# Threshold attention and MLP mixer in one kernel: the residual is turned at the third product and moved every iteration, the ring of turned e gets a fifth place, e two tiles, and the half group adds its residual last

## The chip, the cores and the metric

The kernel runs on one core of one Trainium2 chip. Its time is device time in microseconds (us), from the start of the program to its end. The core has five engines that take their instructions from queues of their own, in order, and wait for each other through semaphores: TensorE (PE; PEld is its loading of weights, which overlaps), VectorE (DVE), ScalarE (ACT), GpSimd (POOL) and SyncE (SP, which here only issues transfers). ACT issues transfers too. An instruction that waits holds back all that stand behind it in its queue.

## What is computed

Eight batches, eight heads, 576 tokens, head size 64. Attention keeps only the scores that lie within tau of the row's maximum; its output goes into a mixer: a product over tokens with a residual, then a product over channels with a residual.

```python
scores = scale * np.matmul(q, k.transpose(0, 1, 3, 2))
thresh = np.max(scores, axis=-1, keepdims=True) - tau
scores = np.where(scores >= thresh, scores, -1000000000.0)
scores = scores - np.max(scores, axis=-1, keepdims=True)
attn = np.exp(scores)
attn = attn / (np.sum(attn, axis=-1, keepdims=True) + 1e-09)
attn_out = np.matmul(attn, v)
x = attn_out.transpose(0, 2, 1, 3).reshape(B, S, H * D)
u = x + (np.maximum(x.transpose(0, 2, 1) @ w_tok1, 0.0) @ w_tok2).transpose(0, 2, 1)
out = u + np.maximum(u @ w_ch1, 0.0) @ w_ch2
```

All is in 32-bit floats.

## The kernel before

**Units.** Attention goes by 144 units, 18 for each batch; a unit is 128 query rows of a pair of heads. The main loop (L758) makes one iteration for each unit u, and in it several units are in work at different stages. `scores(u)` (L311 to L317): PE makes the scores of both heads in PSUM, DVE takes the maxima (`mx`, L316), POOL makes the thresholds (`bias`, L317). `weigh(u)`: ACT reads the scores from PSUM into `e` with Prelu (L326, two instructions) and takes the exponential in place (L333). `norm(u - 1)`: DVE makes the reciprocal of the sums (L340, L341) and POOL scales e (L344). `turn_blocks(u - 2)` (L375), for all batches after the first: DVE transposes e in blocks of 32x32 into the ring `T`. Then, after each third unit, SP issues 16 transfers (L384) that put the ring's blocks into `eT`, and `values` multiplies eT with v on PE (L419, L424) two iterations later. The queue of DVE has in an iteration u: mx of both heads, the two small instructions of L340 and L341, whatever mixer work came in between, and L375 of unit u - 2. L326 of unit u stands behind no instruction of DVE other than mx, but the program has it after `turn_blocks(u - 2)`.

**Tiles of e and the ring.** e has three tiles that go round, so that L326 of unit u writes where unit u - 3 was. The ring T has four places of one unit each; odd threes of units fill it backwards (places 3, 2, 1), even ones forwards (0, 1, 2), so two places are shared by neighbouring threes. The first batch (18 units) has no ring: its e is transposed on PE, and the pool `first` holds an eT for it, which is given back when the ring is made (L761).

**The mixer** runs as filling work between the units: `fill(share)` (L691) takes steps from a list, as much as a running credit allows. Its channel part (`channel_mlp`, L506) goes by groups of 256 tokens, with a half group of 128 after each four: twelve products `ch1(j)` of four matmuls (L532), each put through Relu by ACT into `g` (L533), and then the second product. For full groups that one is a Strassen scheme of seven products of six matmuls each (L568): DVE makes sums of the operands (`sums`, L597, L598, and L613, L621), adds each product to the residual `ut` (`keep`, L582) or makes an output of it in `us` (`give`, L587). The half group has three steps with a scheme of its own (`half_first`, `half_second`, `half_third`). PSUM tiles of these products and of the token products (L459, L469) come from one pool of two (`ps_mm`).

**The residual** must be turned from channels-by-tokens to tokens-by-channels. `turn_u` (L516) transposes 32x32 blocks on DVE into the tile `us`, and 16 transfers (`move`, L522) go from us to `ut`. turn_u is called with `ch1(3)`; the transfers are put into the list `moves`, and SP gets them when `move_u` is called: at the end of an iteration whose unit u - 2 is the first of its three (L850), or at the first step that needs them. `us` has one tile. It is read by the 16 transfers, then holds `S1` of the sums (L597), then the outputs, until the store (L564) has read them; turn_u of the next group waits for that store. `ut` has one tile too.

**Transfers** of SP: loads of v (L116), the eT transfers (L384), the moves (L522) and the stores (L564), in the order in which the program issues them. ACT issues those of q and k (L107) in between its own work. Transfers of both queues take eight completion semaphores in turn, and one that takes a semaphore waits until the transfer that used it before has landed.

Of the kernel before, what the change touches and what calls it, by code (L numbers as in the profile page):

```python
# [9 lines left out]
F32 = mybir.dt.float32  # L10
# [7 lines left out]
P = 128  # L18
# [3 lines left out]
def kernel(  # L22
# [25 lines left out]
    nc = tc.nc  # L48
    B, H, S, D = q.shape
# [14 lines left out]
    NK = 2 * S // P  # L64
# [5 lines left out]
    work = ctx.enter_context(tc.tile_pool(name="work", bufs=2))  # L70
# [6 lines left out]
    first = late.enter_context(tc.tile_pool(name="first", bufs=1))  # L77
    T = None
    ps_3rd = late.enter_context(tc.tile_pool(name="ps_3rd", bufs=1, space=bass.MemoryType.PSUM))
# [8 lines left out]
    UB = 9 * NP // 2  # L88
# [50 lines left out]
    HM = DM // 2  # L139
# [117 lines left out]
    def need(i):  # L257

        weight(3 * i + 4 - steps_done)
# [60 lines left out]
    def weigh(u):  # L320
        sc, bias = st.pop(u)
        rs = small.tile([P, 2], F32, tag="rs", name=f"rs_{u}")
        e = work.tile([P, 2 * S], F32, tag="e", bufs=3, name=f"e_{u}")
        for h in range(2):
            eh = e[:, S * h : S * h + S].rearrange("p (f x) -> p f x", f=2)
            nc.scalar.activation(out=eh, in_=sc[h][:, :, 0:HS], func=AF.Prelu, bias=bias[:, h : h + 1], scale=SCALE, alpha=STEEP)  # L326
        st[u] = e, rs

        if b_now:
            fill(0.2)  # L330
        for h in range(2):
            eh = e[:, S * h : S * h + S]
            nc.scalar.activation(out=eh, in_=eh, func=AF.Exp, bias=ntau, accum_out=rs[:, h : h + 1])  # L333
            if b_now:
                fill(0.2)
# [11 lines left out]
    GU = 3  # L347
# [20 lines left out]
    def turn_blocks(u):  # L368

        b, p0, t = units[u]  # L370
        key, place = (b, p0, t // GU), t % GU
        e = st.pop(u)
        back = (u // GU) % 2
        slot = GU - place if back else place
        nc.vector.transpose(  # L375
            out=T[:, slot].rearrange("p a (c x) -> p c a x", c=NK), in_=e.rearrange("p (c a x) -> p c a x", c=NK, a=4)
        )
        if place == GU - 1:
            eT = work.tile([P, GU, 4, NK * 32], F32, tag="eT", bufs=1, name=f"eT_{u}")
            eTs[key] = eT.rearrange("p n i (c x) -> p (n i) c x", c=NK)  # L380
            slots = slice(GU, 0, -1) if back else slice(0, GU)
            for a in range(4):
                for i in range(4):
                    nc.sync.dma_start(out=eT[32 * a : 32 * a + 32, :, i, :], in_=T[32 * i : 32 * i + 32, slots, a, :])  # L384

# [104 lines left out]
    moves = deque()  # L490
# [15 lines left out]
    def channel_mlp(b, uT, i):  # L506

        s = {}
        n = min(GR, 2 * S - GR * i)
# [16 lines left out]
        def ch1(j):  # L526
            need(7 + j)
            if j == 0:
                s["g"] = work.tile([P, NJ, GR], F32, tag="g", bufs=1, name=f"g_{b}_{i}")
            ps = ps_mm.tile([P, GR], F32, tag="mm", name=f"c1_{b}_{i}_{j}")[:, 0:n]  # L530
            for c in range(NCC):
                nc.tensor.matmul(ps, lhsT=wc1[:, j, c, :], rhs=uT[:, c, GR * i : GR * i + n], start=(c == 0), stop=(c == NCC - 1))  # L532
            nc.scalar.activation(out=s["g"][:, j, 0:n], in_=ps, func=AF.Relu)  # L533
            if j == 3:
                s["us"] = work.tile([P, GR // P, 4, NCC * 32], F32, tag="us", bufs=1, name=f"us_{b}_{i}")
                if not early_rows:
                    s["ut"] = work.tile([P, GR // P, 4, NCC * 32], F32, tag="ut", bufs=1, name=f"ut_{b}_{i}")
                    turn_u()
# [33 lines left out]
        def natural(x):  # L572

            return x.rearrange("q (c k d) -> q c k d", c=NCC // 2, k=4)
# [5 lines left out]
        def keep(t, f, ps):  # L580

            nc.vector.tensor_add(out=rest(t, f), in0=natural(ps), in1=rest(t, f))  # L582

        def give(t, f, ps):

            o = s["us"][:, t].rearrange("q a x -> q (a x)")[:, HM * f : HM * f + HM]
            nc.vector.tensor_add(out=natural(o), in0=natural(ps), in1=rest(t, f))  # L587
# [53 lines left out]
        def p4():  # L641
# [3 lines left out]
            give(1, 0, ps)  # L645
            store(1)

        def half_first():
            move_u()
            s["C"] = ps_mm.tile([P, HM], F32, tag="mm", name=f"C_{b}_{i}")  # L650
            product(s["C"], s["g"][:, 0:HJ, 0:P], B11, True)
            keep(0, 1, s["C"])

        def half_second():
            ps = ps_mm.tile([P, HM], F32, tag="mm", name=f"D_{b}_{i}")
            product(ps, s["g"][:, 0:HJ, 0:P], B12, True, False)
            product(ps, s["g"][:, HJ:NJ, 0:P], B22, False)
            give(0, 1, ps)
            if b == B - 2:
                store(0, slice(HM, DM))  # L660

# [13 lines left out]
        tied.update((p5, p6, p3, p7, p4))  # L675
        return steps + [(2.6, p) for p in (p2, p1, p5, p6, p3, p7, p4)]

    def move_u():
        while moves:
            moves.popleft()()  # L680

# [7 lines left out]
    def fill(share):  # L691
        nonlocal credit
        credit += share * quota
        while todo and credit > 0:
            cost, step = todo.popleft()
            credit -= cost
            step()
        if not todo:
            credit = 0.0
# [58 lines left out]
    for u in range(len(units) + LAG + 4):  # L758
        on = u < len(units)
        if u == UB:  # L760
            late.close()  # L761
            ring = ctx.enter_context(tc.tile_pool(name="ring", bufs=1))
            T = ring.tile([P, GU + 1, 4, NK * 32], F32, name="T")
            ps_mm = ctx.enter_context(tc.tile_pool(name="ps_mm", bufs=2, space=bass.MemoryType.PSUM))
        if on:
            b_now, p0, t = units[u]
            n = b_now * NP + p0
        w = u - LAG
        back = 0 <= w < len(units)
        if on:  # L770
            scores(u)

        last = False
        visit = False
        if due and not in_blocks(due[0][1]):
            visit = due[0][0] <= u
            last = values_due(u)
        elif early:
            early.popleft()[1]()
        if 0 < u <= len(units):  # L780
            norm(u - 1)


        turns_left = b_now and back and not in_blocks(units[w][0])
        if b_now:
            if turns_left:
                weigh(u)
            else:
                weight(2)
        else:  # L790


            weight_to(2.25 * (u - (1 if visit else 1.5)))
            if visit:
                weigh(u)
        while copies:
            copies.popleft()()
        if last and u < UB:
            early.extend(sum(token_mlp(0, range(NP // 2)), []))
        elif last:  # L800
            push(0)
        if back:
            wb, wp, wt = units[w]
            if not in_blocks(wb):
                for i in range(3):
                    turn(w, i)
            if wt % GU == GU - 1:
                g = wt // GU
                if g < 2:
                    split_middle(wb * NP + wp + g)  # L810
                due.append((u + (2 if in_blocks(wb) else 1), wb, wp, g))
        if b_now:
            fill(0.4)
        if back and in_blocks(wb):
            turn_blocks(w)
        if b_now:
            weight(4 if turns_left else 2)
        if turns_left:
            fill(0.6)
        elif on and (b_now or not visit):  # L820
            weigh(u)
        elif b_now:
            fill(0.6)
        if b_now:
            weight(2)
        elif u == 0:
            on_scalar(0, 0)
            on_scalar(0, 1)
        else:
            weight_to(2.25 * (u - 1))  # L830
        if on:


            when = {3: (2, 0, 2), 4: (2, 2, 4), 5: (2, 4, 6), 6: (2, 6, 8), 8: (3, 0, 3), 0: (1, 3, 6), 1: (1, 6, 8)}
            if u == 0:
                load_qk(1, (nc.sync, nc.sync), range(0, 3))
            if t in when:
                m, lo, hi = when[t]
                if n + m < len(pairs):
                    load_qk(n + m, (nc.scalar if b_now else nc.sync,) * 2, range(lo, hi))  # L840
            if t in (2, 5) and 1 < n + 1 + t // 3 < len(pairs):
                load_v(n + 1 + t // 3)
            if t == 2:
                prep(n + 1)
            if t == 7 and n + 2 < len(pairs):
                prep(n + 2)
        if due and in_blocks(due[0][1]):
            values_due(u)

        if back and wt % GU == 0 or not on:  # L850
            move_u()
    need(len(pieces) - 1)
    quota = 1e9
    fill(1.0)
# [28 lines left out]
```

## Time and profile before

| | us |
|---|---|
| median of three runs | 1380.14 (1378.98 to 1380.59) |
| the profiled execution | 1378.7 |
| its span, first to last instruction | 1376.9 |
| PE busy in 0 to 120 (first batch) | 97.9 of 120.0 |
| PE busy in 120 to 325 | 191.9 of 205.0 |
| PE busy in 325 to 1215 (units and mixer together) | 841.4 of 890.0 |
| PE busy in 1215 to 1376.9 (mixer alone) | 158.8 of 161.9 |
| DVE busy in 325 to 1215 | 424.7 |
| ACT busy in 325 to 1215 | 369.9 |

The span is what the profile divides; the execution's own time is 1.8 us longer, and the median of the runs lies 1.4 us above that execution. PE is at work nearly always, so that a change can take little from the kernel but PE's idle stretches and the matmuls that run at a lower clock behind some of them. A group of instructions in the profile has a line, an engine, the tiles written and read, a count, the busy time, the mean of one in ns, and the idle time before them with what ended it. In a timeline a row has its start and its time in us; rows of equal instructions are merged.

### The profile page before, as it was taken

How to read it: one execution, taken by the hardware profiler on the slowest of the kernel's cores; microseconds unless marked ns; L12 is line 12 of the kernel's file. 1: busy time of each engine (PE TensorE's matmuls, PEld its weight loads, DVE VectorE, ACT ScalarE, POOL GpSimd, SP SyncE). 2: the span in 40 equal slices, each digit the busy share in tenths (PEclk: the TensorE clock that was granted, in tenths of full speed). 3: DMA queues.
4: the chain of work that ended last, by engine and by line, in shares of the span. 5: the costliest groups of instructions: out<-in, count | busy, mean ns of one | idle time of the engine just before them, and what ended most of it. 6: DMA issues, size and time to landing. Idle time of an engine off the chain costs nothing.

```text
span 1376.9 us, 19588 instructions
## 1 busy us (share of the span) xinstructions
PE 1290.0 (94%) x6882; PEld 955.7 (69%) x6882; DVE 669.7 (49%) x1176; ACT 585.6 (43%) x1320; POOL 372.3 (27%) x695
## 2 busy tenths in 40 slices
PE   8888999989899989999999899999999969999999
PEld 5555646557676867677777677678777756778888
DVE  6878864454555533655355445545454534402211
ACT  6776655345354434453434444353425524220110
POOL 4565643225322221222222223122222312100000
PEclk8999999999999999999999999999999989999999
DMA  5535764545354434453343535444444532320010
GB/s 112 120 94 132 197 155 104 118 104 112 93 133 107 113 90 105 115 120 92 87 111 89 123 83 129 110 98 105 109 95 102 129 79 60 78 72 16 16 31 32
DMA packets 300082, 136.74 MB, mean 99 GB/s; under 512 B 205584, under 2 KB 292880, under 8 KB 299984
## 3 DMA queue, kind: packets, MB, share of 16 engines
q1 hardware_dynamic: 172272, 119.58, 34.0%
q10 hardware_dynamic: 127712, 15.90, 7.3%
q8 instruction: 55, 0.90, 0.3%
q14 instruction: 43, 0.35, 0.1%
HBM read 43.25 MB, written 9.44 MB: 38 GB/s over the span
## 4 chain that ended last, share of the span: by engine, by line
PE 67%; SPq 10%; DVE 8%; DMA 6%; ACT 4%; issue 2%; POOL 1%; ACTq 0%; DVEq 0%; POOLq 0%
PE c L532 22%; PE sc L311 9%; PE D L568 7%; PE pv L424 7%; PE C L568 7%; SPq L522 5%; SPq L384 5%; PE t L459 5%; PE t L469 4%; DVE mx L316 3%; PE c L553 2%; PE pv L419 2%; DMA lq<-in_q_dram 2%; ACT e L326 2%; DMA lk<-in_k_dram 1%
## 5 line engine op out<-in xcount | busy, mean ns | idle before, releaser
L532 PE MATMUL c<-xT,wc 128*128 128x256 f32 (+1 forms) x1920 | 399.9, 362 | 1.0 <-ACT g L533 1.0
L532 PEld LDWEIGHTS c<-xT,wc 128*128 128x128 f32 x1920 | 333.7, 191 | 62.2 <-issue 21.3
L316 DVE TENSOR_REDUCE mx<-sc 128x1 f32<-128x576 f32 x288 | 204.2, 750 | 294.2 <-PE sc L311 293.1
L317 POOL TENSOR_SCALAR bias<-mx,toff 128x1 f32<-128x1 f32 x288 | 81.6, 284 | 782.3 <-DVE mx L316 727.0
L326 ACT ACTIVATE e<-sc,bias 128x576 f32<-128x576 f32 x288 | 199.2, 740 | 193.7 <-POOL bias L317 187.7
L344 POOL TENSOR_SCALAR e<-e,rr 128x576 f32<-128x576 f32 x288 | 219.7, 775 | 15.0 <-DVE rr L341 3.5
L333 ACT ACTIVATE e<-e,ntau 128x576 f32<-128x576 f32 x288 | 221.3, 772 | 0.0
L375 DVE STREAM_TRANSPOSE T<-e 128x1152 f32<-128x1152 f32 x126 | 172.1, 1366 | 72.2 <-DMA eT<-T 49.9
L533 ACT ACTIVATE g<-c 128x256 f32<-128x256 f32 (+1 forms) x240 | 87.3, 364 | 280.2 <-PE c L532 264.2
L311 PE MATMUL sc<-kT,qT 64*128 64x288 f32 (+1 forms) x1280 | 193.1, 436 | 5.5 <-ACT e L326 5.3
L311 PEld LDWEIGHTS sc<-kT,qT 64*128 64x128 f32 (+1 forms) x1280 | 106.0, 179 | 79.4 <-issue 42.3
L424 PE MATMUL pv<-eT,lv 128*64 128x384 f32 (+1 forms) x1024 | 141.4, 417 | 0.0
L424 PEld LDWEIGHTS pv<-eT,lv 128*64 128x64 f32 x1024 | 78.4, 140 | 51.8 <-issue 44.0
L429 ACT COPY xT<-pv 128x384 f32<-128x384 f32 (+1 forms) x56 | 21.0, 401 | 183.4 <-PE pv L424 183.4
L568 PE MATMUL C<-wx,g 128*128 128x256 f32 x336 | 78.6, 384 | 3.9 <-DVE g L613 3.9
L469 PE MATMUL t<-w,a 128*128 128x288 f32 x256 | 74.2, 421 | 6.9 <-DVE xT L473 6.8
L459 PE MATMUL t<-x_sb,w 128*128 128x256 f32 x320 | 76.4, 386 | 1.5 <-ACT x_sb L453 1.5
L568 PE MATMUL D<-wc,g 128*128 128x256 f32 x264 | 62.3, 389 | 16.5 <-ACT a L461 14.0
L568 PEld LDWEIGHTS C<-wx,g 128*128 128x128 f32 x336 | 62.8, 190 | 17.6 <-DVE g L613 6.5
L459 PEld LDWEIGHTS t<-x_sb,w 128*128 128x128 f32 x320 | 59.7, 192 | 14.0 <-issue 3.9
L568 PEld LDWEIGHTS D<-wc,g 128*128 128x128 f32 x264 | 50.5, 194 | 26.7 <-ACT a L461 14.8
L568 PE MATMUL C<-wc,g 128*128 128x256 f32 x264 | 62.9, 389 | 2.9 <-DVE ut L582 2.9
(72 smaller groups left out, 1094.0 us busy)
## 6 DMA issues: line engine op xcount, KB each, us to landing
eT<-T SPq DMA_DIRECT2D x672, 108.0 KB, 2.3
scratch<-in_moe_w_ch_dram SPq DMA_DIRECT2D x24, 512.0 KB, 3.7
lv<-in_v_dram SPq DMA_DIRECT2D x32, 288.0 KB, 3.4
out_dram<-us SPq DMA_DIRECT2D x35, 256.0 KB, 2.2
lk<-in_k_dram ACTq DMA_DIRECT2D x109, 72.0 KB, 2.8
lq<-in_q_dram ACTq DMA_DIRECT2D x106, 72.0 KB, 2.4
ut<-us SPq DMA_DIRECT2D x224, 32.0 KB, 1.9
lk<-in_k_dram SPq DMA_DIRECT2D x19, 72.0 KB, 3.2
```

Source lines behind the costliest of these rows:

```text
L311: nc.tensor.matmul(sc[h][rows, f, 0:HS], lhsT=qT[r, cols], rhs=kT[r, HS * f : HS * f + HS], start=True, stop=True)
L316: nc.vector.tensor_reduce(out=mx[:, c], in_=sc[h][:, :, 0:HS], axis=AX.XY, op=ALU.max)
L326: nc.scalar.activation(out=eh, in_=sc[h][:, :, 0:HS], func=AF.Prelu, bias=bias[:, h : h + 1], scale=SCALE, alpha=STEEP)
L333: nc.scalar.activation(out=eh, in_=eh, func=AF.Exp, bias=ntau, accum_out=rs[:, h : h + 1])
L344: nc.gpsimd.tensor_scalar(out=eh, in0=eh, scalar1=rr[:, h : h + 1], scalar2=1.0, op0=ALU.mult, op1=ALU.mult)
L375: nc.vector.transpose(out=T[:, slot].rearrange("p a (c x) -> p c a x", c=NK), in_=e.rearrange("p (c a x) -> p c a x", c=NK, a=4))
L424: nc.tensor.matmul(to[r], lhsT=lv[:, j, :], rhs=e[j], start=False, stop=(c == NI - 1), skip_group_check=True)
L459: nc.tensor.matmul(to, lhsT=w1[:, t, P * m : P * m + P], rhs=x_sb[:, t, xs], start=(t == 0), stop=(t == NT - 1))
L469: nc.tensor.matmul(to, lhsT=a[:, m, P * (c - ps[0]) : P * (c - ps[0]) + P], rhs=w2[:, m, HS * f : HS * f + HS], start=(m == 0), stop=(m == ...
L532: nc.tensor.matmul(ps, lhsT=wc1[:, j, c, :], rhs=uT[:, c, GR * i : GR * i + n], start=(c == 0), stop=(c == NCC - 1))
L533: nc.scalar.activation(out=s["g"][:, j, 0:n], in_=ps, func=AF.Relu)
L568: nc.tensor.matmul(to, lhsT=left[:, j, :], rhs=right[:, j, :], start=(start and j == 0), stop=(stop and j == HJ - 1), skip_group_check=True)
```

## The change

Five edits:

1. `turn_u` is called with `ch1(2)` instead of `ch1(3)`.
2. `move_u` is called at the end of every iteration. Where unit u - 2 is the second of its three, it issues at most six transfers, and the rest with the next call.
3. The ring T has five places; threes that go backwards fill places 4, 3, 2, so neighbouring threes share place 2 alone.
4. e has two tiles in `work`. In the first batch, odd units take theirs from `first`, which has two more.
5. In the half group, ACT copies the first product to an unused half of us (`spare`); DVE adds the second product to it and then adds the residual. Before, DVE added the residual to the first product at once.

```diff
-        e = work.tile([P, 2 * S], F32, tag="e", bufs=3, name=f"e_{u}")
+        e = (first if u < UB and u % 2 else work).tile([P, 2 * S], F32, tag="e", bufs=2, name=f"e_{u}")
...
-        slot = GU - place if back else place
+        slot = 2 * GU - 2 - place if back else place
...
-            slots = slice(GU, 0, -1) if back else slice(0, GU)
+            slots = slice(2 * GU - 2, GU - 2, -1) if back else slice(0, GU)
...
-            if j == 3:
+            if j == 2:
                 s["us"] = work.tile([P, GR // P, 4, NCC * 32], F32, tag="us", bufs=1, name=f"us_{b}_{i}")
...
+        def spare():
+            return s["us"][:, 1].rearrange("q a x -> q (a x)")[:, 0:HM]
+
         def half_first():
             move_u()
             s["C"] = ps_mm.tile([P, HM], F32, tag="mm", name=f"C_{b}_{i}")
             product(s["C"], s["g"][:, 0:HJ, 0:P], B11, True)
-            keep(0, 1, s["C"])
+            nc.scalar.copy(out=spare(), in_=s["C"])
 
         def half_second():
             ps = ps_mm.tile([P, HM], F32, tag="mm", name=f"D_{b}_{i}")
             product(ps, s["g"][:, 0:HJ, 0:P], B12, True, False)
             product(ps, s["g"][:, HJ:NJ, 0:P], B22, False)
-            give(0, 1, ps)
+            nc.vector.tensor_add(out=spare(), in0=ps, in1=spare())
+            give(0, 1, spare())
...
-    def move_u():
-        while moves:
+    def move_u(n=100):
+        while moves and n > 0:
             moves.popleft()()
+            n -= 1
...
-            T = ring.tile([P, GU + 1, 4, NK * 32], F32, name="T")
+            T = ring.tile([P, 2 * GU - 1, 4, NK * 32], F32, name="T")
...
-        if back and wt % GU == 0 or not on:
-            move_u()
+        move_u(6 if back and wt % GU == 1 else 100)
```

## The prediction

> **What bounds the kernel.** I read, in this order, the page's shares, the waits of PE and DVE, SP's own waits, and the timeline around each long wait.
>
> ```profile
> PE 1290.0 (94%) x6882; PEld 955.7 (69%) x6882; DVE 669.7 (49%) x1176; ACT 585.6 (43%) x1320; POOL 372.3 (27%) x695
> ...
> DVE T L375 <- DMA eT<-T: 49.9, 17, 5.5
> ...
> DVE ut L582 <- DMA ut<-us: 44.0, 3, 16.3
> DVE us L597 <- DMA ut<-us: 43.1, 7, 10.3
> ...
> PE D L568 <- ACT a L461: 14.0, 2, 13.5
> ...
> PE D L568 <- DVE us L597: 9.9, 6, 2.6
> PE pv L419 <- DMA eT<-T: 9.7, 6, 3.6
> ...
> SPq L522 <- DMA lq<-in_q_dram: 42.4, 10, 7.2
> ```
>
> PE works 94% of the span, so only its gaps can be won, and some 27 us of them lie in the first batch, which the change hardly touches. After 325 us they are 46 us. DVE waits 49.9 us for ring places and 87.1 us for the residual's transfers, but PE stands still behind that for much less: 9.9 us for the sums, 9.7 us for eT, and the 13.5 us put down to `a`. The next rows show that this last one is the residual as well.
>
> ```profile
> 1085.43 1.36 DVE L375 STREAM_TRANSPOSE T<-e 128x1152 f32<-128x1152 f32 x1
> 1086.86 12.48 SPq L384 DMA_DIRECT2D eT<-T  x16
> 1090.50 1.36 DVE L375 STREAM_TRANSPOSE T<-e 128x1152 f32<-128x1152 f32 x1
> 1099.44 0.53 SPq L564 DMA_DIRECT2D out_dram<-us  x1
> 1101.68 0.71 DVE L516 STREAM_TRANSPOSE us<-xT 128x512 f32<-128x512 f32 x1 [3.62 <-DMA out_dram<-us]
> ...
> 1121.24 10.11 SPq L522 DMA_DIRECT2D ut<-us  x16
> 1132.98 0.42 DVE L582 TENSOR_TENSOR ut<-C,ut 128x256 f32<-128x256 f32 x1 [16.34 <-DMA ut<-us]
> ...
> 1137.51 6.86 PE L568 MATMUL D<-wc,g 128*128 128x256 f32 x24 [13.49 <-ACT a L461]
> ```
>
> In this half group keep waits 16.34 us on DVE for transfers that SP issues behind 16 of eT. Maxima, Prelu and at last the freeing of a PSUM tile (`a`) queue behind it, and PE stands 13.49 us.
>
> **Part 1, the half group (edits 2 and 5), a gain of 20.0.** The copy (0.38 us, as other ACT copies of that size) waits for no transfer, and the moves go out ahead of an eT, not behind it. DVE gets one more addition (0.42 us), off PE's path, as half_third's six matmuls follow. Gone: the 13.49 and the slow matmuls after it (24 in 6.86 instead of 5.18: 1.7), and in the half group at 501 us the 2.92 and 12 matmuls in 4.52 instead of 2.59 (1.9). In the others (807, 1368 us) PE doesn't wait. Bounds: 15 to 20.
>
> **Part 2, earlier transfers (edits 1 and 2), a gain of 25.** In four full groups (ready at 421, 543, 868 and 1188 us) six moves now pass 16 eT transfers; the other ten end some 4 us sooner at 0.65 us an issue. Gone there: 1.74, 2.32, 2.10 + 0.93, 2.61 + 1.95 (12 matmuls in 4.54), and 1.33 before values at 1213 us: 13.0. In the others the moves pass one load only (0.55 us). But the 42.4 us in which SP holds a move for a q load that ACT hasn't issued shrink, as a move mostly waits for such a load later in its sixteen by the new program (in the group at 337 us the fourth, not the second; in that at 728 us the tenth, not the seventh). PE's gaps there are 8.1 (356 to 368 us, slow matmuls counted), 2.6 (691 to 700), 4.8 (752 to 768) and 1.25 (1017): 16.8. I take 12 of them. Bounds for the part: 13 to 30. The price: a move now stands in front of eT, but in all four cases SP's queue is empty then.
>
> **Part 3, the store wait (edit 1), a loss of 15.** Who is late next? Turning earlier moves L516 one iteration up the queue of DVE, where us must have been stored. In the half groups at 464 and 1102 us the store stands behind 16 eT transfers. In the rows above L516 would follow the transpose that ends at 1091.9; the store is issued at 1099.44 and L516 could start at 1101.68. Behind it wait mx, L375, and through them Prelu, ACT's Relu copies, and PE, which may run ahead by two PSUM tiles. Prelu would start at about 1101.7 + 0.7 + 1.4 + 0.4 + 1.4 = 1105.5 and the next Relu end at 1107.3; PE reached the product that needs that tile at 1100.1: 7.2 lost, and 1.7 for slow matmuls. At 464 us the same sum (transpose ends 454.3, L516 at 464.5, values at 470.3 instead of 464.1) gives 6.2 and 1.9. Together 17.0; the store may come 2 us sooner if the 16 transfers take 0.65 each and not 0.78: I take 15. Bounds: 0 (something else covers it) and 17. In the other groups the store has landed, or DVE has idle time.
>
> The trace has half-speed matmuls after gaps of 2.35, 2.61, 2.92 and 3.58 us, none after 2.10 and 2.32. The Trainium skill ("TensorE: Matmul & The Clock Gate", section "Why this matters for your kernels") puts the bound at gaps of about 3 us, and so speaks against any edit that makes a gap like the two of part 3. By it the gaps of 2.35, 2.61 and 2.92 would cost no clock, and parts 1 and 2 would be some 5.5 us smaller; I follow the rows.
>
> **Part 4, two tiles of e (edit 4), a loss of 16.5 + 6.6.** L326 of unit u now waits for L375 of unit u - 2, of the same iteration. Behind it in ACT's queue stand the exponentials and the Relu copies, and the next scores on PE wait for the PSUM that it frees. In 116 of 124 iterations that transpose ends after Prelu's start in the trace, at the median by 1.8 us.
>
> ```profile
> 209.46 1.42 DVE L316 TENSOR_REDUCE mx<-sc 128x1 f32<-128x576 f32 x2 [4.46 <-PE sc L311]
> 210.61 1.40 ACT L326 ACTIVATE e<-sc,bias 128x576 f32<-128x576 f32 x2 [1.81 <-POOL bias L317]
> 211.08 1.36 DVE L375 STREAM_TRANSPOSE T<-e 128x1152 f32<-128x1152 f32 x1
> 212.11 1.24 PE L311 MATMUL sc<-kT,qT 64*128 64x288 f32 x8
> ```
>
> Here Prelu starts 1.82 us before the transpose ends (212.44). The second Prelu ends at 212.01, and scores that wait for Prelu start 0.58 before its end (the first head is free by then), so the slack is 212.11 - 212.01 + 0.58 = 0.68, and PE loses 1.14. The same subtraction for each iteration, ring waits left out as edit 3 takes them, gives, by the transpose's start: 0.57 (131), 0.86 (159), 0.75 (166), 0.55 (174), 1.64 (186), 0.63 (190), 1.14 (211), 0.21 (232), 1.13 (262), 0.21 (325), 0.23 (346), 1.74 (383), 0.21 (405), 2.95 (433), 0.38 (448), 0.79 (504), 1.85 (557), 2.03 (754), 1.31 (773), 1.13 (1150), 20.3 in all. At 433 and 557 the iteration was late only through sums that part 2 frees; I take off 3.8: 16.5. Where PE fills an iteration with ch1, there is slack of 0.45 (Relu copy done 669.2, its tile needed at 669.65), and nothing is lost. Bounds: 11 to 35 (without the 0.58).
>
> Five transposes stand behind sums that wait for the residual: 5.31 (358), 4.99 (692), 4.41 (749), 6.72 (877), 3.35 (1011), together 24.8 if it lands no sooner. With part 2's 4.2, 3.0, 2.0, 5.9 and 3.0 us off, what remains is 1.1, 2.0, 2.4, 0.8 and 0.3: 6.6.
>
> **Part 5, the ring's fifth place (edit 3): 0.** It takes DVE's 49.9 us, but PE's waits for eT stand behind late issues on SP, not behind place waits. Its cover is PE's own work; without it up to 49.9 would count, at worst nothing is gained.
>
> **Sum.** -20.0 - 25.0 + 15.0 + 16.5 + 6.6 = -6.9. The profiled execution took 1378.7 (span 1376.9 and 1.8 around it), so 1371.8; the median of the runs lies 1.4 above it: 1373.
>
> **Rivals.** *ACT behind the transpose has no slack* (slower): part 4's first term is 35 instead of 16.5, the sum +11.6, 1392. It decides from about 26 on. For it: ACT and DVE both turn in each iteration's chain, and 116 of 124 have the new wait last. Against it: scores do start before the second Prelu's end (557.35 is one that waits for Prelu). *The transfers land no sooner* (the change doesn't do what it says): SP still waits for ACT's q loads, which come later behind the new wait. Part 2 gives 13, the five transposes cost 24.8, of which 5 fall into gaps that PE had: -20 - 13 + 15 + 16.5 + 19.8 = +18.3, 1398. For it: 42.4 us of such waits. Against it: most of them move to later transfers of the sixteen. *The store wait is hidden*: part 3 at 0, -21.9, 1358. For it: in the trace L516 waited 3.6 us there and PE only 1.0. Against it: the wait becomes 10 us.
>
> **Chances.** Forecast 0.50 (its own range 1363 to 1380), no slack 0.22, no sooner 0.13, store hidden 0.15. Range 1358 to 1394: it leaves out the far part of the third. What can't be told from no change is within 0.2% (2.8 us): faster takes 0.43 of the forecast's half and the last case, 0.57 with some taken off; same 0.05; slower 0.38 (the two slow rivals and the forecast's upper end).
>
> **What would show it.** The waits of T for eT gone, and L582 in the half groups no longer waiting for ut; L516 waiting some 10 us for the store twice, near 455 and 1090 us, with a PE gap of 6 to 7 behind each; L326 ended by L375 in most iterations; the sums' wait at 5 to 15 us instead of 43.1. If PE's waits for Prelu (5.3 us) rise past 30, the forecast is wrong on the slow side; if L516's waits leave PE alone, on the fast side.

## The result, and the profile after

The changed kernel takes 1412.86 us (median of 4 runs, 1410.5 to 1416.5) against 1380.37 of the kernel before in the same comparison: a ratio of 1.0236, 95% interval 1.021 to 1.0263. It is slower by 32 us, where I forecast 1373 and a range that ended at 1394.

The first two lines are from the page of the kernel before, the others from the page of the changed kernel (busy times by engine; then groups: busy time and mean ns of one, then idle time of the engine before them and what ended most of it).

```profile
L326 ACT ACTIVATE e<-sc,bias 128x576 f32<-128x576 f32 x288 | 199.2, 740 | 193.7 <-POOL bias L317 187.7
...
L311 PE MATMUL sc<-kT,qT 64*128 64x288 f32 (+1 forms) x1280 | 193.1, 436 | 5.5 <-ACT e L326 5.3
```

```profile
PE 1313.4 (93%) x6882; PEld 970.7 (69%) x6882; DVE 674.0 (48%) x1176; ACT 586.3 (42%) x1324; POOL 371.7 (26%) x695
...
L326 ACT ACTIVATE e<-sc,bias 128x576 f32<-128x576 f32 x288 | 198.3, 738 | 336.5 <-DVE T L375 281.5
...
L311 PE MATMUL sc<-kT,qT 64*128 64x288 f32 (+1 forms) x1280 | 213.8, 448 | 36.6 <-ACT e L326 34.6
...
L375 DVE STREAM_TRANSPOSE T<-e 128x1152 f32<-128x1152 f32 x126 | 172.2, 1366 | 5.2 <-POOL bias L317 4.0
```

The waits of the engines in the changed kernel (us in total, times, longest):

```profile
PE sc L311 <- ACT e L326: 34.6, 26, 4.5
...
PE pv L419 <- DMA ut<-us: 7.0, 1, 7.0
PE c L532 <- ACT g L533: 6.5, 1, 6.5
...
DVE us L516 <- DMA out_dram<-us: 39.1, 9, 11.2
...
DVE us L597 <- DMA ut<-us: 35.3, 9, 8.8
...
SPq L384 <- DMA lq<-in_q_dram: 45.7, 17, 5.2
...
SPq L522 <- DMA lq<-in_q_dram: 41.1, 11, 6.6
```

Much is as the forecast wanted it: L375's ring waits of 49.9 us are gone, no keep (L582) of a half group waits for ut any more, and the two store waits are there with a PE gap behind each (7.0 and 6.5 us). But Prelu (L326), which waited for the bias before, is now ended by L375 for 281.5 us, and PE waits 34.6 us for it instead of 5.3, past the 30 that the prediction named as the sign of its being wrong on the slow side. And the busy time of the scores (L311), whose 1280 matmuls are the same, has grown from 193.1 to 213.8 us: a stall that lies between the matmuls of one unit is counted as busy. So the page's wait is not the whole loss. To have both, I took for each unit from 18 on the time from the end of PE's instruction before its scores to the end of its last score matmul, and summed: 157.0 us in the kernel before, 206.6 in the changed one.

### The profile page after: what moved, and what is told of

It is laid out like the page before. It is cut to its first block, busy times and chain, and to the rows that moved or that the text cites. A ratio compares the mean times of both kernels' runs of the same rounds, so it can differ in the third digit from the quotient of the medians.

```text
span 1408.7 us, 19765 instructions
## 1 busy us (share of the span) xinstructions
PE 1313.4 (93%) x6882; PEld 970.7 (69%) x6882; DVE 674.0 (48%) x1176; ACT 586.3 (42%) x1324; POOL 371.7 (26%) x695
## 4 chain that ended last, share of the span: by engine, by line
PE 73%; DVE 9%; SPq 5%; ACT 5%; DMA 4%; issue 2%; POOL 1%; ACTq 0%; DVEq 0%; POOLq 0%
PE c L532 22%; PE sc L311 12%; PE D L568 9%; PE C L568 7%; PE pv L424 7%; PE t L459 4%; PE t L469 4%; SPq L384 3%; DVE mx L316 3%; DVE T L375 3%; ACT e L326 3%; PE pv L419 2%; SPq L522 2%; PE c L553 2%; DMA lq<-in_q_dram 1%
## 5 line engine op out<-in xcount | busy, mean ns | idle before, releaser
L532 PEld LDWEIGHTS c<-xT,wc 128*128 128x128 f32 x1920 | 335.6, 192 | 70.7 <-issue 20.1
L326 ACT ACTIVATE e<-sc,bias 128x576 f32<-128x576 f32 x288 | 198.3, 738 | 336.5 <-DVE T L375 281.5
L311 PE MATMUL sc<-kT,qT 64*128 64x288 f32 (+1 forms) x1280 | 213.8, 448 | 36.6 <-ACT e L326 34.6
L344 POOL TENSOR_SCALAR e<-e,rr 128x576 f32<-128x576 f32 x288 | 216.2, 763 | 15.7 <-DVE rr L341 3.9
L311 PEld LDWEIGHTS sc<-kT,qT 64*128 64x128 f32 (+1 forms) x1280 | 116.2, 183 | 119.1 <-ACT e L326 61.1
L375 DVE STREAM_TRANSPOSE T<-e 128x1152 f32<-128x1152 f32 x126 | 172.2, 1366 | 5.2 <-POOL bias L317 4.0
L424 PE MATMUL pv<-eT,lv 128*64 128x384 f32 (+1 forms) x1024 | 139.1, 414 | 0.0
L424 PEld LDWEIGHTS pv<-eT,lv 128*64 128x64 f32 x1024 | 78.1, 141 | 51.1 <-issue 43.3
L469 PEld LDWEIGHTS t<-w,a 128*128 128x128 f32 x256 | 46.5, 193 | 25.2 <-DVE xT L473 7.0
```

What stands on the lines that cost most here:

```text
L311: nc.tensor.matmul(sc[h][rows, f, 0:HS], lhsT=qT[r, cols], rhs=kT[r, HS * f : HS * f + HS], start=True, stop=True)
L344: nc.gpsimd.tensor_scalar(out=eh, in0=eh, scalar1=rr[:, h : h + 1], scalar2=1.0, op0=ALU.mult, op1=ALU.mult)
L375: nc.vector.transpose(out=T[:, slot].rearrange("p a (c x) -> p c a x", c=NK), in_=e.rearrange("p (c a x) -> p c a x", c=NK, a=4))
L424: nc.tensor.matmul(to[r], lhsT=lv[:, j, :], rhs=e[j], start=False, stop=(c == NI - 1), skip_group_check=True)
L469: nc.tensor.matmul(to, lhsT=a[:, m, P * (c - ps[0]) : P * (c - ps[0]) + P], rhs=w2[:, m, HS * f : HS * f + HS], start=(m == 0), stop=(m == ...
```

## The experiments

Behind each measured time stands its ratio to the kernel before, with its 95% interval. An interval's half is about 3 us (5 for x1, 4 for x15), so a difference of two medians is good to some 4 to 5.

**Which of the edits loses it.** Four kernels, each made of some of the edits.

*x1: edits 3 and 4 alone* (on the kernel before, with the ring's size and slots to match).

```diff
-        e = work.tile([P, 2 * S], F32, tag="e", bufs=3, name=f"e_{u}")
+        e = (first if u < UB and u % 2 else work).tile([P, 2 * S], F32, tag="e", bufs=2, name=f"e_{u}")
...
-        slot = GU - place if back else place
+        slot = 2 * GU - 2 - place if back else place
```

> The kernel before with edits 3 and 4 alone: two tiles of e, five places in the ring, the residual turned and moved as before. Theory A (the two tiles of e were priced too low; PE loses some 50 us to Prelu behind L375, about 29 of it as waits and 20 inside stretched scores): 1415 to 1432, with L326 ended by L375 for over 250 us and L311's busy time near 210 us instead of 193.1. Theory B (the turn one product earlier, with its wait for the store and the moves in front of eT, is what the changed kernel lost by): at most 1395, L311 near 195 us. By my recorded prices it would be 1380 + 20.3 + 24.8 - 5 = 1420, since here the five sums stay late; so the time alone can't clear the first term of part 4, the waits by iteration have to.

Measured: 1453.20 us, 1.0544 (1.0507 to 1.058). Even above theory A: 73 us lost (71.5 between the two profiled spans, 1448.4 and 1376.9, of which the sum at the scores shows 226.6 - 157.0 = 69.6). L326 is ended by L375 for 332.0 us, L311's busy time is 215.3.

*x2: the changed kernel without edits 3 and 4* (the two hunks above taken back, with the ring's size).

> The changed kernel without edits 3 and 4: three tiles of e, four places. Theory A: the loss goes with the two tiles, so about 1413 - 50 = 1363, range 1352 to 1375, PE's waits for Prelu back to some 5 us, L311's busy time near 193 us. Theory B: the loss stays, 1395 or more. Theory C (the transfers land no sooner, so edit 2 gives 13 and not 25): 1380 - 20 - 13 + 15 = 1362 against 1350 by the recorded prices; A and C together 1358 to 1366. The waits of T for eT (49.9 us before) may grow, as six moves now stand in front of some eT.

Measured: 1357.21 us, 0.9838 (0.9814 to 0.9861): faster than before by 23, and 55.7 below the changed kernel. Theory B falls. Whether part 2 gives 25 or 13 (theory C) isn't told here: 1357 lies between the two sums. On the page of this kernel:

```profile
L326 ACT ACTIVATE e<-sc,bias 128x576 f32<-128x576 f32 x288 | 199.1, 739 | 172.0 <-POOL bias L317 163.2
...
L311 PE MATMUL sc<-kT,qT 64*128 64x288 f32 (+1 forms) x1280 | 193.4, 438 | 6.0 <-ACT e L326 4.3
```

Prelu is back behind the bias, and both parts of the scores' loss, the wait and the stretch, are gone; the sum at the scores is 154.5, so 52.0 of the loss lie there. The two profiled spans (1408.7 and 1357.0) differ by 51.7, so in them the scores account for all of it; the other 4 of the 55.7 are within what two medians can tell.

*x3: edit 5 alone* (with `spare` as in the change).

```diff
-            keep(0, 1, s["C"])
+            nc.scalar.copy(out=spare(), in_=s["C"])
...
-            give(0, 1, ps)
+            nc.vector.tensor_add(out=spare(), in0=ps, in1=spare())
+            give(0, 1, spare())
```

> The kernel before with edit 5 alone: the half group's first part is copied by ACT and the residual added last; turn, moves and tiles as before. By part 1 the wait of keep (16.3 us) and PE's 13.5 us behind it go, 15 to 20 in all: 1360 to 1366. If the wait only moves to the added sum one step later and holds the maxima again: 1372 to 1380.

Measured: 1360.59 us, 0.9863 (0.984 to 0.9886), 19.5 below before. Part 1 stands, and edit 5 does it without edit 2.

*x4: edits 2 and 5* (x2 with the residual turned at the fourth product again).

```diff
-            if j == 2:
+            if j == 3:
```

> Edits 2 and 5 alone: three tiles of e, four places, the residual turned at the fourth product as before, its moves issued every iteration. Theory A with part 3 as priced: this is the last kernel without the store wait of the two half groups, so 13 to 17 below it if the moves land as early, 1343 to 1352. If the earlier turn is what lets the moves pass eT: the same as the last or slower, 1358 to 1372.

Measured: 1354.06 us, 0.9808 (0.9781 to 0.9836), between the two expectations. Against x3, edit 2 gives 6.5; against x2, edit 1 as a whole costs 3, which can't be told from nothing.

**Is it the number of tiles, or where L375 stands?**

*x5: the changed kernel, L375 ahead of the scores.*

```diff
+        if back and in_blocks(units[w][0]):
+            turn_blocks(w)
         if on:
             scores(u)
...
-        if back and in_blocks(wb):
-            turn_blocks(w)
```

> The changed kernel with all five edits, and one line moved: L375 of unit u - 2 is issued ahead of the scores of unit u, so that it stands in DVE's queue before the maxima of u (and before the sums that wait for the residual), in time in which DVE waits for PE. Theory A1 (the two tiles cost time only because L375 stands behind the maxima and the sums in DVE's queue, so that Prelu comes a transpose or a late sum later): of the 52 us that PE loses at the scores 40 or more come back, 1352 to 1372, and L326 is ended by the bias again. Theory A2 (two tiles are too few in any order, since e is still being divided and turned when the next Prelu wants it): 1395 to 1415, L326 ended by L375 or by POOL.

Measured: 1345.29 us, 0.9749 (0.9725 to 0.9773): 67.6 below the changed kernel, more than was asked for. From its page:

```profile
L326 ACT ACTIVATE e<-sc,bias 128x576 f32<-128x576 f32 x288 | 199.3, 739 | 176.8 <-POOL bias L317 176.4
...
L375 DVE STREAM_TRANSPOSE T<-e 128x1152 f32<-128x1152 f32 x126 | 172.4, 1369 | 65.6 <-POOL e L344 52.2
```

With the same two tiles Prelu waits for the bias alone. L375 now waits, for POOL, but in time in which DVE had waited for PE. DVE's wait of mx for the scores, first in the changed kernel, then here:

```profile
DVE mx L316 <- PE sc L311: 375.5, 115, 9.8
...
DVE mx L316 <- PE sc L311: 240.2, 82, 6.9
```

So two tiles are enough; what cost was that L375 stood behind mx and the sums in DVE's queue. The moves wait for q loads as long as in the changed kernel (45.4 us), so their waits are not what went. The sum at the scores is 153.3.

*x6: the same with the turn at the fourth product* (as x4's hunk).

> As the last, with the residual turned at the fourth product (edit 1 undone). With A1, and the store wait of the half groups worth 10 to 14: 1340 to 1362, 3 to 14 below the last. With A2: 1390 to 1412.

Measured: 1339.92 us, 0.971 (0.9687 to 0.9732), 5.4 below x5, little more than the noise.

*x7: x4 with L375 ahead of the scores* (three tiles, four places).

> Edits 2 and 5, three tiles of e and four places in the ring, L375 issued ahead of the scores. Here L375 waits 48.7 us for places in the ring, and in this order the maxima wait behind it: theory D (edits 3 and 4 belong together, and the fifth place is what lets L375 stand early): slower than the same kernel in the old order, 1360 to 1395. If those waits fit into DVE's idle time before the maxima (300 us): 1345 to 1356.

Measured: 1348.51 us, 0.9771 (0.9746 to 0.9795): theory D falls: though L375 waits 45.6 us for the ring, the kernel is not slower than in the old order (x4) but 5.5 faster. x6 is this kernel with edits 3 and 4, and it is 8.6 us faster: in this order two tiles and five places are better than three and four. Where the 8.6 lie was not followed; the sums at the scores are alike (156.0 and 155.4).

*x8: x4 with the early turn in the full groups only.*

```diff
-            if j == 3:
+            if j == (2 if n == GR else 3):
```

> Edits 2 and 5 with three tiles of e, and edit 1 in the full groups only; the half groups turn the residual at the fourth product. If edit 1 costs by the store wait in the half groups (two gaps of 5.2 us in the kernel with edit 1 throughout) and gains in the full ones: 1343 to 1351, below both of its neighbours (1354 and 1357). If the full groups gain nothing: 1352 to 1356.

Measured: 1340.43 us, 0.9723 (0.9697 to 0.975), below both expectations. It is 13.6 below x4, what edit 1 gains in full groups, and 16.8 below x2, what it costs in half groups. Timeline of x8, the store and the turn in the two half groups that part 3 is about (start, duration, idle time before with its releaser):

```profile
458.72 0.53 SPq L564 DMA_DIRECT2D out_dram<-us  x1
...
461.07 0.71 DVE L516 STREAM_TRANSPOSE us<-xT 128x512 f32<-128x512 f32 x1 [3.65 <-DMA out_dram<-us]
...
1077.86 0.53 SPq L564 DMA_DIRECT2D out_dram<-us  x1
...
1080.10 0.71 DVE L516 STREAM_TRANSPOSE us<-xT 128x512 f32<-128x512 f32 x1 [3.49 <-DMA out_dram<-us]
```

One iteration later the turn waits 3.65 and 3.49 us for the store, in the changed kernel 11.17 and 10.18.

**The best order, and the fifth place.**

*x9: x8 with L375 ahead of the scores from unit 38 on* (the new position `if u >= 38`, the old one `if u < 38`).

> Edits 2 and 5, edit 1 in the full groups only, three tiles of e, four places, and L375 issued ahead of the scores from unit 38 on, where the preparation of the weights on DVE and POOL has ended. In the kernels with L375 first throughout, two gaps of 5.4 to 7.5 us (at 155 and 185 us, Relu behind Prelu behind late maxima) come with the weights; without them and without the store wait this goes below all kernels so far: 1320 to 1335. If the order gives nothing beyond what the moves gave: 1338 to 1343.

Measured: 1336.14 us, 0.9683 (0.9659 to 0.9707), just outside what I hoped for. The two gaps at 155 and 185 us are gone (none over 1.4 us between 139 and 225 us), but the gain over x8 is only 4.3.

*x10: the same with all five edits* (edit 1 in full groups).

> The changed kernel (five edits) with edit 1 in the full groups only and L375 ahead of the scores from unit 38 on. Up to there the two tiles cost what they cost the changed kernel (11 us at unit 36), after it the fifth place of the ring takes the waits of L375 for places: 1325 to 1345; above the last one if the early units weigh more, below if the places do.

Measured: 1335.95 us, 0.9684 (0.9662 to 0.9706), the same as x9: in this order the time is the same with three tiles and four places, or two and five. At the scores x10 loses 10.9 us more (166.9 against 156.0), all before unit 38, where L375 still stands in its old place; what makes up for it was not followed.

*x11: x5 with the early turn in the full groups only.*

> The changed kernel with L375 ahead of the scores throughout and edit 1 in the full groups only. Against the same kernel with edit 1 everywhere (1345) the store wait of the half groups goes (gap of 4.1 us at 1082 us, and Relu waits of 18.4 us in all): 1334 to 1342.

Measured: 1340.49 us, 0.9715 (0.9693 to 0.9736), 4.8 below x5. In this order the store wait costs some 5 and not 16.8, and the early turn in full groups gains nothing that can be measured (x6 has 1339.92); the reason was not followed up.

*x12: the changed kernel without edit 3.*

```diff
-        slot = 2 * GU - 2 - place if back else place
+        slot = GU - place if back else place
...
-            T = ring.tile([P, 2 * GU - 1, 4, NK * 32], F32, name="T")
+            T = ring.tile([P, GU + 1, 4, NK * 32], F32, name="T")
```

> The changed kernel without edit 3: two tiles of e, four places. By part 5 (worth 0) 1408 to 1418. If L375's waits for places (36 to 50 us with three tiles) now hold Prelu too, as two tiles make Prelu wait for L375: 1420 to 1450.

Measured: 1397.42 us, 1.0131 (1.011 to 1.0151): neither. The kernel is 15.4 faster without the fifth place. Its waits of SP (L375 waits for the ring again, 24.0 us in all):

```profile
SPq L384 <- DMA lq<-in_q_dram: 39.4, 17, 4.1
...
SPq L522 <- DMA lq<-in_q_dram: 6.1, 3, 3.1
```

The moves' waits for q loads fell from 41.1 to 6.1 us. A move that takes one of the eight completion semaphores waits for the transfer that had it before; by the traces, 33 of the 288 moves of the changed kernel (and 33 of x2's) take theirs from a load that ACT issues, in this one 16. What that does in one group is seen by two timelines, first the changed kernel:

```profile
690.69 18.12 SPq L522 DMA_DIRECT2D ut<-us  x16
...
692.28 0.32 ACTq L107 DMA_DIRECT2D lq<-in_q_dram  x1
...
698.84 0.32 ACTq L107 DMA_DIRECT2D lq<-in_q_dram  x1
...
710.51 0.96 DVE L597 TENSOR_TENSOR us<-g 128x768 f32<-128x768 f32 x1 [5.45 <-DMA ut<-us]
...
712.72 1.37 DVE L375 STREAM_TRANSPOSE T<-e 128x1152 f32<-128x1152 f32 x1
...
714.18 1.37 ACT L326 ACTIVATE e<-sc,bias 128x576 f32<-128x576 f32 x2 [8.50 <-DVE T L375]
...
714.97 2.92 PE L311 MATMUL sc<-kT,qT 64*128 64x288 f32 x8 [4.54 <-ACT e L326]
```

and the same group without the fifth place:

```profile
691.26 10.72 SPq L522 DMA_DIRECT2D ut<-us  x16
...
703.65 1.02 DVE L597 TENSOR_TENSOR us<-g 128x768 f32<-128x768 f32 x1 [1.63 <-DMA ut<-us]
```

Sixteen moves take 18.12 us in the one and 10.72 in the other; in the first the sums wait 5.45 us, L375 stands behind them, Prelu waits 8.50 us for it, PE 4.54.

**Were those waits the cause?** x12 changed the place and the waits together, so here are three more.

*x13: the changed kernel with q and k loaded by SP.*

```diff
-                    load_qk(n + m, (nc.scalar if b_now else nc.sync,) * 2, range(lo, hi))
+                    load_qk(n + m, (nc.sync, nc.sync), range(lo, hi))
```

> The changed kernel, with the loads of q and k issued by SP instead of ACT, so that no transfer of SP can wait for a load that ACT has not issued. If those waits (41.1 us in front of the moves, 45.7 us in front of eT) are what kept the residual late, the five iterations lose 2 to 3 us each and not 4 to 6: 1394 to 1403 like the kernel without the fifth place (1397). If the fifth place itself costs: 1408 to 1416. SP has 213 more transfers to issue, so loads can also come later and take some of it back.

Measured: 1399.59 us, 1.0141 (1.0121 to 1.0161), as x12, with the fifth place kept. In the scores of units 51, 89, 95, 110 and 125, which wait for a Prelu behind late sums, the excess over x2 is 4.97 + 6.28 + 3.65 + 2.74 + 3.92 = 21.6 us in the changed kernel, 7.8 in x12 and 7.4 here.

*x14: the kernel before with the same loads.*

> The kernel before with the loads of q and k issued by SP. Its moves wait 42.4 us for ACT's loads, and PE stands 16.8 us in groups with such moves (of which I took 12 as won by part 2): 1364 to 1374. If PE's waits there have other causes: 1377 to 1384.

Measured: 1367.64 us, 0.9907 (0.9889 to 0.9924): moving the loads gains 12.9 in the kernel before.

*x15: x9 with the same loads.*

> The kernel with L375 first from unit 38 on and three tiles of e (1336), with the loads of q and k issued by SP. Its moves wait 25.2 us and eT 20.9 us for such loads, but PE waits little for either: 1328 to 1338.

Measured: 1326.92 us, 0.9601 (0.9572 to 0.963): a little below what was expected and the fastest of all, 53.6 below the kernel before and 86 below the changed one.

## Why the prediction was wrong

By the differences of the runs, in us:

| step | forecast | measured | from |
|---|---|---|---|
| part 1, half group | -20.0 | -19.5 | x3 less before |
| part 2, earlier transfers | -25.0 | -20.1 | (x4 less x3) -6.5, (x8 less x4) -13.6 |
| part 3, store wait | +15.0 | +16.8 | x2 less x8 |
| part 4, two tiles of e | +23.1 | +40.2 | x12 less x2 |
| part 5, fifth place | 0 | +15.4 | changed less x12 |
| sum | -6.9 | +32.8 | |

(The sum misses the 32.5 between the two kernels by 0.3, as the runs are from several comparisons.) The last two rows depend on their order. x12 has few of the moves' waits (6.1 us), x2 and the changed kernel have them alike (41.8 and 41.1 us, 33 such moves in each). So parts 4 and 5 together are 55.7 at equal waits, and the 40.2 is the price of the two tiles with most of those waits gone.

**Part 1** and **part 3** were right in mechanism and size. Part 2 as a whole lies within its bounds of 13 to 30, but 12 of its 25 were to come from the moves waiting less for ACT's loads. They wait as long as before (40.5 us in x4, 42.9 in x8, 42.4 before), so that the size is near is partly luck; what shrank in x8 is the sums' wait, from 43.1 to 18.7 us. The store wait came where it was worked out: at 464 and 1102 us of the old clock, the two PE gaps were forecast with 6.2 and 7.2 us. Timeline of the changed kernel at the first:

```profile
480.57 0.53 SPq L564 DMA_DIRECT2D out_dram<-us  x1
...
482.88 0.71 DVE L516 STREAM_TRANSPOSE us<-xT 128x512 f32<-128x512 f32 x1 [11.17 <-DMA out_dram<-us]
...
485.09 1.36 DVE L375 STREAM_TRANSPOSE T<-e 128x1152 f32<-128x1152 f32 x1
486.54 1.37 ACT L326 ACTIVATE e<-sc,bias 128x576 f32<-128x576 f32 x2 [7.46 <-DVE T L375]
...
487.80 0.58 ACT L453 COPY x_sb<-tx 128x512 f32<-128x512 f32 x1
...
488.44 0.91 PE L419 MATMUL pv<-eT,vl 128*64 128x192 f32 x4 [7.01 <-DMA ut<-us]
...
489.13 2.77 PE L424 MATMUL pv<-eT,lv 128*64 128x192 f32 x16
...
492.33 1.53 PE L424 MATMUL pv<-eT,lv 128*64 128x192 f32 x16
```

Store, turn, transpose, Prelu, PE: the chain of part 3, link by link, and the slow matmuls behind it (16 in 2.77 us, then 16 in 1.53). The view puts PE's wait down to a move, but PE starts at 488.44, just behind the end of ACT's copy L453 (487.80 + 0.58), which stands behind Prelu and frees the PSUM tile. Of the prediction's row of gaps with and without slow matmuls one was overlooked: in the kernel before, a gap of 2.09 us that ends at 292.46 has slow matmuls behind it too (those of L424 take 0.85 us each, where most of that form take 0.50). So the length of the gap alone doesn't tell. And PE's gaps after 325 us, read as 46 us, sum to 48.3; nothing rests on that figure.

**Part 4's first term is the first failure**, above all in one figure: the credit of 0.58 us. I had seen that scores which wait for Prelu start 0.58 us before the second Prelu's end, and took that as slack in each iteration. They do start there, but the matmuls of a unit go to both heads in turn, and the second of them has to wait for the second head after all. Timeline of the changed kernel:

```profile
448.94 1.37 ACT L326 ACTIVATE e<-sc,bias 128x576 f32<-128x576 f32 x2 [4.68 <-DVE T L375]
...
449.74 1.87 PE L311 MATMUL sc<-kT,qT 64*128 64x288 f32 x8 [0.91 <-ACT e L326]
```

The scores start 0.57 us before the second Prelu's end (448.94 + 1.37 = 450.31), and the eight matmuls take 1.87 us, where eight take 1.24 unhindered: 0.63, the credit, is paid inside the scores and counted as busy. In 18 units the matmuls of the scores take 0.55 to 0.63 us longer than in x2. Behind the long gap at 714.97 they take 2.92, as there the single matmuls are slower too (the last six at 0.68 us each, not 0.40). Of the 20 iterations of my list 18 lost time, in the scores of the next unit, 25.7 us in all; eight others lost 4.7. Together 30.4, where I took 20.3 after the credit and 3.8 off that; the list's 20.3 with 20 times 0.58 put back is 31.9. One by one it fits less well: behind the listed transposes at 166 and 186 no time is lost. The bound of 35 that I gave, and its rival, were nearer than the 16.5.

**Part 4's second term, with part 2, is the second failure.** I let the five transposes behind late sums cost 6.6 because part 2 would bring the residual sooner by shrinking the 42.4 us of moves that wait for ACT's q loads. They stayed at 41.1, the sums' wait, forecast at 5 to 15, is 35.3, and the five cost 21.6. I had counted by the order of semaphores in which transfer of the sixteen a move would meet a load, and took a later place as a shorter wait. But all sixteen must land before the sums start: a load that is met late in the sixteen holds the last of them as long as one met early. In the group above the seventh move goes out at 702.47, when ACT's load issued at 698.84 has landed (702.45). In x12 and x13, where the waits are nearly or wholly gone, the sums wait 11.3 and 15.0 us and the five cost 7.8 and 7.4, close to the 6.6. These waits alone don't do it, though: with three tiles (x2) the moves wait 41.8 us for loads as well, and the sums only 16.0. That the loads come later behind the new wait of Prelu, as the rival said, would fit; it was not measured by itself. What the same waits cost the kernel before, put at 12 in part 2, fits the 12.9 of x14; only it was not the change that took them away.

**Part 5**, put at 0, lost 15.4. Most of it comes from the semaphores that the transfers happen to get: 13.7 of it (21.56 - 7.84) lie in those five iterations, which lose as little in x13, with the place and without the waits. That a ring's size can do this was not in my list at all. Whether the place itself costs anything isn't shown apart: x13 with it takes 1399.6 and x12 without it 1397.4, but in x13 the loads come from another queue too, and at the scores it sums to 196.7 where x12 has 188.8. Why the program hands out its semaphores differently with another place was not traced.

**The rivals.** I had "no slack" (1392) and "transfers land no sooner" (1398) as alternatives. At the scores both came true at once, as both act through one wait, L326 behind L375, which stands behind the maxima in the one and behind late sums in the other: 30.4 and 21.6 us, together 52.0, where their terms were 35 and 19.8, together 54.8. The second rival's other half didn't come: part 2 gave 20.1, not 13.

## What to carry to other kernels

When a tile of a ring is taken away, look at what stands ahead of the instruction that frees it in its queue, and move that instruction into idle time first: the two tiles and the fifth place together cost 55.7 us with the transpose behind the maxima and the sums, and with the transpose ahead of them they gain 8.6 (x6 against x7). A stall between the matmuls of one group is hidden in PE's busy time; compare the busy time of the group, not only its waits, and take the difference within the profiled executions, not the medians. Rivals that act through the same wait can come together; price their sum too.

## What was not expected of the hardware

Transfers of one engine can be held by the loads of another through shared completion semaphores. Without it the kernel before is 12.9 us faster (x14) and the changed one some 13 (x13); the moves had waited 41 to 42 us in each, and the transfers of eT 17.2 and 45.7. Moving 213 loads from ACT's queue to SP's cost nothing that outweighed it, though DVE then waits 55.8 us for q (x13). PE's busy time rose by 20.7 us in the scores with the count and kind of its matmuls unchanged; most of it is waiting between them, some of it slower matmuls behind long gaps.
